# First pass of a fused retention, ELU and GLU kernel: one d_ff block of the first two half groups moved to the pass's end, retention two steps further ahead, four x stores issued by ScalarE

## The chip, the cores and the metric

The kernel runs on one core of one Trainium2 chip. The metric is the device time of one execution in microseconds (us). Engines are named as in the profile: PE (TensorE), DVE (VectorE), ACT (ScalarE), POOL (GpSimd), SP (SyncE). An engine works through its own instructions in the order in which they stand. The execution that was profiled is one execution; the times are the median of several.

## The reference, cut to what matters

```python
# retention: batch 4, heads 8, seq 576, head_dim 64
scores = q @ k.T / sqrt(64);  ret = scores * gamma_h ** (i - j)  (0 where j > i)
x = (ret @ v), heads side by side          # 2304 tokens x 512
h = x @ w_in                               # 512 -> 2048
x = where(h > 0, h, exp(min(h, 0)) - 1) @ w_out
gate = sigmoid(x @ w_gate)                 # 512 -> 1536
out = (gate * (x @ w_val)) @ w_out2
```

All weights come as 64-bit words (float64) and are turned into pairs of float32 on the chip. Every large product is made of three PE products of high and low parts.

## The kernel before

**Tokens and groups.** 2304 tokens are 18 retention steps of 128 tokens. Steps 0 to 3 make token group 0, 4 to 7 group 1, and so on; group 4 has two steps. A half group is 256 tokens, two steps. The 2048 columns of d_ff are 16 blocks of 128.

**First pass.** `FP = 2`: the first pass takes d_ff blocks 0 and 1 for all nine half groups, 18 FF steps `s` in the list `ff`. Step `s = 2j + f` is half group `j`, block `f`. `ff[s].ups` is 12 products on PE into a bank `h` (L369), then on ACT Relu and Exp (L382, L383), on DVE a combination (L386), on ACT the high part of the result `g` (L108) and on DVE or POOL its low part (L109). `ff[s - 2].downs` (`LAG = 2`) is 12 products into two accumulator banks (L113 to L115), and after the last block of a half group `evac` copies them to `y`.

**Retention.** Between the FF steps stands `block(n)`: on PE `inter` of step n, `scores` of step n + 1, `outs` of n, `sums` of n + 1, 64 products of 64x64 in float32, which are 128 matrix products and 128 weight loads in the trace (L263). On DVE follow `causal` (L275, the mask of scores n + 1), `x_mul` (L336, the output x of step n out of the bank `to`), the two halves of `states` (L297, L301, the state of step n + 1; POOL L302 and L260 scale it and the next v), and `x_low` (L350); ACT makes `x_high` (L343). `inter` of step n + 1 waits for the second half of `states`, so from one block to the next there is a chain PE, `x_mul`, `states`, PE. `x_low` also stores the float32 x of groups 0 to 3 to memory (L354), read again in later passes. `x_mul` of step n writes one of two tiles `e`, so it waits for the store of step n - 2.

**Weights.** `chain` of a Weight is five stages: two ACT operations (L153, L154), two DVE (L156, L157), DVE L160, DVE L162, then ACT L168 for the high part and DVE or POOL L171 for the low part. `stages(w, n)` runs n of them where it stands; in a FF step `stage()` does.

**Order.** It is written out by hand (`manual_schedule`). Before, `AHEAD = 2`: at step s from 4 on `block(s + 2)` runs ahead of `ups`; steps 0 to 3 have an order of their own, with warm-up products on PE (L121) in between. SP issues nearly all transfers, in program order; it also holds an empty instruction (L317) between `inter` and `outs` of a step, for which PE waits.

The second pass begins at s = 18 with group 4 and adds to the same `y`; later passes follow. The lines that set the order in the first pass:

```python
            if LATE <= s < NSTEP - AHEAD:
                block(s + AHEAD)
            ...
            ff[s].ups(stage, s, middle, end_)
            ...
            if s >= LAG:
                ff[s - LAG].downs(stage)
```

Of the kernel before, what the change touches and what calls it, by code (L numbers as in the profile page):

```python
# [24 lines left out]
NT = B * S  # L25
# [5 lines left out]
NSTEP = (B // 2) * NS  # L31
# [7 lines left out]
KEPT = 3  # L39
SEVEN = 5  # L40
N0 = 256
AHEAD = 2
LATE = 4
SPARE = {3: 2, 8: 2, 4: 3, 9: 3, 14: 3}
LAG = 2
WARM = 12, 2, 3, 5, 4, 6


LEAST = float(np.array(0x38000000, np.uint32).view(np.float32))
# [4 lines left out]
def retention_elu_glu(  # L54
# [25 lines left out]
    class Ring:  # L80
# [5 lines left out]
        def more(self, pool, n):  # L86
            self.homes += [(pool, f"{self.name}{len(self.homes) + i}") for i in range(n)]
# [87 lines left out]
    def t_slot(n, f):  # L175
        if n == "i":
            return f % 2 + 3 * (f > 5 and f % 4 < 2)
        return 2 if not f % 2 or f == 2 * Q0 + 1 else 0 if f == FA - 1 else 5

    W, weights = {}, []  # L180
    for f in range(FA):
        for n, src in (("i", w_in), ("o", w_out)):
            i = len(weights)
            W[n, f] = Weight(src[f], i % 8, (0, 0, 1, 1, 0, 1, 0, 1)[i] if i < 8 else t_slot(n, f))
            weights.append(W[n, f])


# [35 lines left out]
    class Step:  # L223
# [125 lines left out]
        def x_low(self):  # L349
            dve.tensor_tensor(out=self.x[1], in0=self.xf, in1=self.x[0].bitcast(F32), op=ALU.subtract)  # L350
            if self.g < 4:
                if not self.at:
                    whole[self.g] = dpool.tile([128, KB, 512], F32, tag=f"x{self.g}", name="x")
                sp.dma_start(out=whole[self.g][:, :, self.at : self.at + 128], in_=self.xf)  # L354


    class FF:
# [425 lines left out]
    with tc.manual_schedule():  # L783
# [33 lines left out]
        steps[0].load()  # L817
        weights[0].load()
        steps[1].load()
        weights[2].load()  # L820
        steps[2].load()
        steps[3].load()
        weights[1].load(raws[:, 0, :])
        steps[4].load()
        weights[3].load(raws[:, 1, :])

# [5 lines left out]
        def block(n, scales=True):  # L832

            more = n + 1 < NSTEP
            steps[n].inter()
            if more:
                steps[n + 1].scores()
            steps[n].outs()
            if more:
                steps[n + 1].sums()  # L840
                steps[n + 1].causal()
            for load in loads_at.get(n, []):
                load()
            steps[n].x_scaled()
            if more:
                steps[n + 1].states()
                if scales and n + 2 < NSTEP:
                    steps[n + 2].scale()
            steps[n].x_low()

        def stages(chain, n):
            for _ in range(n):
                next(chain)


        w0, w2 = weights[0].chain(dve, apart=True), weights[2].chain(dve)
        warm_up(WARM[0])
        steps[0].scale()
        steps[0].scores()
# [18 lines left out]
        steps[1].causal()  # L878
        steps[1].states()
        steps[0].x_low()  # L880
        stages(w2, 2)
        warm_up(3)
        steps[1].inter()
        steps[1].outs()
# [2 lines left out]
        steps[1].x_high()  # L887
        stages(w0, 1)
        steps[1].x_low()
        stages(w2, 2)  # L890
        for load in loads_at[1]:
            load()
        for X in range(2):
# [2 lines left out]


        passes = [list(range(f, f + FP)) for f in range(0, 2 * Q0, FP)]
        ff = [FF(0, j // 2, f, passes[0], j % 2 * N0, N0) for j in range(NT // N0) for f in passes[0]]
        begins = [0, len(ff)]  # L900
        ff += [FF(1, g, f, passes[1]) for g in (4, 2, 3, 0, 1) for f in passes[1]]
        end = len(ff)

        a, b = begins
        conv, loads = {2: weights[3]}, {}
        for i, w in enumerate(weights[4:8]):
            s = a + 6 + (i * (b - a - 6)) // 4
            conv[s] = w
# [147 lines left out]
        for s in range(end):  # L1056
            if halves is not None:
                next(halves, None)
            chain = halves = None
            if s in conv:  # L1060
                chain = halves = made[name_of[id(conv[s])]] = convert(conv[s])
                if conv[s] is W["i", 2 * Q0 + 2]:
                    halves = None
                if conv[s] is W["i", 2 * Q0]:
                    chain = halves = islice(chain, 4)
            if s == b:
                chain = made["i", 2 * Q0]

            def stage():
                if chain is not None:  # L1070
                    next(chain, None)
                if s >= begins[1] + 4:
                    next(prepared, None)
            stage()
            if LATE <= s < NSTEP - AHEAD:
                block(s + AHEAD)
            if s == NSTEP - AHEAD:
                more()
            middle = end_ = None
            if s == 0:  # L1080
                def middle():
                    stages(w2, 1)
                    steps[2].scores()
                    steps[2].sums(True)
                    steps[2].causal()

                def end_():
                    steps[2].states()
                    steps[3].scale()
                    steps[4].scale()  # L1090
            ff[s].ups(stage, s, middle, end_)
            if s == 1:
                w1 = weights[1].chain(dve)
                block(2, False)
                stages(w1, 2)
                warm_up(WARM[4])
                steps[3].inter()
                steps[4].scores()
                steps[3].outs()
                steps[3].x_mul()  # L1100
                steps[4].sums()
                steps[4].causal()
                steps[3].x_high()
                steps[5].scale()
                stages(w1, 1)
                steps[3].x_low()
                steps[4].states()
                stages(w1, 2)
                for load in loads_at.get(3, []):
                    load()  # L1110
                warm_up(WARM[5])
            if 1 < s < LATE:
                block(s + AHEAD)
            for w in loads.get(s, []):
                w.load()
            if s >= LAG:
                ff[s - LAG].downs(stage)
            else:
                stage()
            save()  # L1120
            for i, n in enumerate(("11", "21", "22")):
                if s == begins[1] + 2 + i:
                    second.store(n)
            if s == begins[1] + 8:
                park()
                more()
            if s == begins[1] + LAG - 1:
                ret.close()
                right = ctx.enter_context(tc.tile_pool(name="right", bufs=1, side="right"))
                e_tile.more(right, 3)  # L1130
                e_tile.n = 5
                g_tile.more(right, 2)
                t_tile.more(right, 1)
                s_tile = Ring("s", right, 2, [128, 2, 2, DM], F32R)
                ps_acc = ctx.enter_context(tc.tile_pool(name="ps_acc", bufs=1, space=bass.MemoryType.PSUM))
                ps_u = ctx.enter_context(tc.tile_pool(name="ps_u", bufs=1, space=bass.MemoryType.PSUM))
                acc_bank = Ring("acc", ps_acc, 4, [128, 512], F32)
                u_bank = Ring("u", ps_u, 2, [128, 512], F32)
# [296 lines left out]
```

## Time and profile before

| | us |
|---|---|
| runs | 889.15, 889.76, 886.13 (median 889.15) |
| profiled execution | 885.46 |
| its span, first to last instruction | 883.7 |
| PE busy in the span | 861.0 |
| DVE, ACT, POOL busy | 664.9, 460.1, 410.2 |

PE is busy for 97% of the span. The first pass, which the change rewrites, ends at about 123.5 us, where the products of the second pass's first step start; 760 us follow. The warm-up products count as busy PE but compute nothing.

### The profile page before, as it was taken

To read this page: it belongs to the slowest core of one execution; us is meant where nothing else is said; L and a number is where in the kernel's file an instruction comes from. 1 tells how busy PE (TensorE), PEld (TensorE's weight loads), DVE (VectorE), ACT (ScalarE), POOL (GpSimd) and SP (SyncE) were. 2 spreads that over 40 slices of the span, in tenths; PEclk is the share of its full clock that TensorE was granted. 3 is DMA by queue.
4 is the path that set the end of the run, shared out by engine and by line. 5 is a ranking of instruction groups with operands and counts; after the bars stand their busy time and mean duration, and the time that the engine had idled before them with its cause. 6 is when DMAs were issued, how large, how long until landed. Compare 5 with 4: busy or idle time off the path is not lost.

```text
span 883.7 us, 16178 instructions
## 1 busy us (share of the span) xinstructions
PE 861.0 (97%) x6370; PEld 729.2 (83%) x6375; DVE 664.9 (75%) x967; ACT 460.1 (52%) x833; POOL 410.2 (46%) x327
## 2 busy tenths in 40 slices
PE   7898999999999999999899999999999999999998
PEld 4798897788888888888788888888888888888886
DVE  5867649679999888887787989479966554786774
ACT  3445475677666656666564565455534334344331
POOL 2446435556556542555361566245434143334353
PEclk9999999999999999999999999999999999999999
DMA  9978528735565595997783766555565565554322
GB/s 342 295 229 271 151 57 311 300 121 190 191 197 209 214 402 201 329 354 273 279 329 113 258 232 227 194 187 186 200 243 186 197 232 194 211 211 179 114 117 96
DMA packets 63724, 194.83 MB, mean 220 GB/s; under 512 B 9760, under 2 KB 18976, under 8 KB 57248
## 3 DMA queue, kind: packets, MB, share of 16 engines
q1 hardware_dynamic: 62544, 192.31, 61.1%
q10 hardware_dynamic: 1104, 1.49, 0.5%
q8 instruction: 50, 0.82, 0.4%
q14 instruction: 26, 0.21, 0.1%
HBM read 127.19 MB, written 66.58 MB: 219 GB/s over the span
## 4 chain that ended last, share of the span: by engine, by line
PE 82%; DVE 8%; ACT 4%; DMA 3%; issue 2%; POOL 1%; SPq 0%; DVEq 0%; ACTq 0%; POOLq 0%
PE u L113 13%; PE u L115 13%; PE u L114 13%; PE acc L113 9%; PE acc L114 9%; PE acc L115 9%; PE tile L113 4%; PE tile L114 4%; PE tile L115 4%; PE to L263 3%; PE h L369 1%; DVE t L157 1%; DMA h<-x 1%; DVE t L156 1%; DMA raw<-in_w_in 1%
## 5 line engine op out<-in xcount | busy, mean ns | idle before, releaser
L109 POOL TENSOR_TENSOR g<-e,g 128x512 fp32r<-128x512 f32 x95 | 132.7, 1402 | 234.3 <-ACT g L108 219.8
L113 PE MATMUL u<-x,s 128*128 128x512 f32 x288 | 114.8, 398 | 3.0 <-DVE e L538 2.5
L115 PE MATMUL u<-x,s 128*128 128x512 f32 x288 | 114.5, 398 | 0.0
L114 PE MATMUL u<-x,s 128*128 128x512 f32 x288 | 114.1, 396 | 0.0
L113 PE MATMUL u<-x,w 128*128 128x512 f32 (+1 forms) x264 | 98.4, 373 | 0.5 <-DVE u L524 0.5
L114 PE MATMUL u<-x,w 128*128 128x512 f32 (+1 forms) x264 | 98.3, 372 | 0.0
L115 PE MATMUL u<-x,w 128*128 128x512 f32 (+1 forms) x264 | 97.8, 371 | 0.0
L108 ACT CAST g<-e 128x512 fp32r<-128x512 f32 x101 | 61.9, 620 | 60.7 <-DVE e L579 39.9
L171 POOL TENSOR_TENSOR w<-t,w 128x512 fp32r<-128x512 f32 x37 | 51.7, 1398 | 41.6 <-ACT w L168 38.9
L113 PEld LDWEIGHTS u<-x,s 128*128 128x128 f32 x288 | 54.3, 189 | 15.5 <-DVE e L538 3.1
L115 PEld LDWEIGHTS u<-x,s 128*128 128x128 f32 x288 | 54.4, 189 | 13.2
L114 PEld LDWEIGHTS u<-x,s 128*128 128x128 f32 x288 | 54.5, 189 | 12.0
L113 PE MATMUL acc<-g,w 128*128 128x512 f32 (+1 forms) x176 | 60.8, 345 | 2.5 <-ACT y L422 1.5
L114 PE MATMUL acc<-g,w 128*128 128x512 f32 (+1 forms) x176 | 60.2, 342 | 0.0
L115 PE MATMUL acc<-g,w 128*128 128x512 f32 (+1 forms) x176 | 60.1, 341 | 0.0
L776 DVE TENSOR_TENSOR y<-y,acc 128x512 f32<-128x512 f32 x58 | 39.1, 682 | 27.5 <-PE acc L115 27.3
L740 DVE TENSOR_TENSOR y<-y,tile 128x512 f32<-128x512 f32 x76 | 51.2, 680 | 10.5 <-PE tile L115 10.2
L113 PEld LDWEIGHTS u<-x,w 128*128 128x128 f32 x264 | 49.8, 189 | 9.4 <-DVE u L524 1.1
L115 PEld LDWEIGHTS u<-x,w 128*128 128x128 f32 x264 | 49.8, 188 | 9.0
L114 PEld LDWEIGHTS u<-x,w 128*128 128x128 f32 x264 | 49.9, 189 | 7.8
L656 DVE TENSOR_TENSOR y<-y,acc 128x512 f32<-128x512 f32 (+1 forms) x68 | 39.6, 606 | 19.7 <-PE acc L115 17.9
L114 PE MATMUL acc<-w,g 128*128 128x512 f32 (+1 forms) x152 | 54.4, 358 | 0.0
(216 smaller groups left out, 2410.0 us busy)
## 6 DMA issues: line engine op xcount, KB each, us to landing
w<-c SPq DMA_DIRECT2D x72, 512.0 KB, 6.4
c<-w SPq DMA_DIRECT2D x48, 512.0 KB, 4.9
s<-c SPq DMA_DIRECT2D x22, 1024.0 KB, 6.4
c<-s SPq DMA_DIRECT2D x18, 1024.0 KB, 4.9
in<-in_ain SPq DMA_DIRECT2D x12, 1024.0 KB, 7.4
y<-y SPq DMA_DIRECT2D x8, 1024.0 KB, 6.2
raw<-in_w_in SPq DMA_DIRECT2D x12, 512.0 KB, 5.4
c<-x SPq DMA_DIRECT2D x12, 512.0 KB, 6.8
```

The costliest lines, as they stand in the source:

```text
L108: act.copy(hi, src)
L109: lo_engine.tensor_tensor(out=lo, in0=src, in1=hi.bitcast(F32), op=ALU.subtract)
L113: pe.matmul(out_, wh, xh, start=start, stop=False, skip_group_check=shared)
L114: pe.matmul(out_, wh, xl, start=False, stop=False, skip_group_check=shared)
L115: pe.matmul(out_, wl, xh, start=False, stop=stop, skip_group_check=shared)
L156: dve.tensor_scalar(out=f, in0=f, scalar1=LEAST, scalar2=MOST, op0=ALU.max, op1=ALU.min)
L157: dve.tensor_scalar(out=u, in0=u, scalar1=5, scalar2=2, op0=ALU.logical_shift_left, op1=ALU.logical_shift_right)
L171: lo_engine.tensor_tensor(out=w[:, 1, :], in0=f, in1=w[:, 0, :].bitcast(F32), op=ALU.subtract)
L263: return pe.matmul(out_, w, x, start=start, stop=True, skip_group_check=True)
L656: dve.tensor_tensor(out=out_, in0=out_, in1=a, op=ALU.add)
L740: dve.tensor_tensor(out=y, in0=y, in1=a, op=ALU.add)
L776: dve.tensor_tensor(out=o, in0=o, in1=a, op=ALU.add)
```

## The change

The list `ff` now has block 0 alone for half groups 0 and 1 (steps 0 and 1), then both blocks for half groups 2 to 8 (steps 2 to 15), then block 1 for half groups 0 and 1 as two steps at the end (16 and 17), with pass number 2: their `evac` adds to `y` on DVE, 128x256 at a time, where the first pass copies on ACT. `AHEAD = 4`, so blocks 2 to 5 stand in steps 0 and 1, blocks 6 to 17 ahead of `ups` in steps 2 to 13, and none in steps 14 to 17. The weight converted ahead of the first FF step is now block 0 of w_out (w1) in place of block 1 of w_in (w2), and w1 is loaded before it; w2 follows in steps 0 and 1, w3 at step 3 in place of 2. Of two groups of warm-ups, of four and six, the one of four stays. The x stores of steps 0 to 3 are issued by ACT, behind `x_high`, and those of later steps by SP as before. One line fewer stands at the top, so a line of the change has a number lower by one down to the reordered part.

```diff
-AHEAD = 2
-LATE = 4
+AHEAD = 4
-WARM = 12, 2, 3, 5, 4, 6
+WARM = 12, 2, 3, 5, 4, 1
...
-                sp.dma_start(out=whole[self.g][:, :, self.at : self.at + 128], in_=self.xf)
+                (act if self.n < 4 else sp).dma_start(out=whole[self.g][:, :, self.at : self.at + 128], in_=self.xf)
...
         steps[1].load()
-        weights[2].load()
+        weights[1].load(raws[:, 0, :])
         steps[2].load()
         steps[3].load()
-        weights[1].load(raws[:, 0, :])
+        weights[2].load()
...
-        ff = [FF(0, j // 2, f, passes[0], j % 2 * N0, N0) for j in range(NT // N0) for f in passes[0]]
+        halves = lambda P, js, fs: [FF(P, j // 2, f, fs, j % 2 * N0, N0) for j in js for f in fs]
+        ff = halves(0, (0, 1), [0]) + halves(0, range(2, NT // N0), passes[0]) + halves(2, (0, 1), [1])
...
-            if LATE <= s < NSTEP - AHEAD:
+            if 1 < s < NSTEP - AHEAD:
                 block(s + AHEAD)
...
+            if s == 1:
+                block(4)
+                stages(w2, 1)
...
             ff[s].ups(stage, s, middle, end_)
+            if s == 0:
+                block(2, False)
+                warm_up(WARM[4])
+                block(3)
+                stages(w2, 2)
             if s == 1:
-                w1 = weights[1].chain(dve)
-                block(2, False)
-                stages(w1, 2)
-                warm_up(WARM[4])
-                steps[3].inter()
-                ...
-                warm_up(WARM[5])
-            if 1 < s < LATE:
-                block(s + AHEAD)
+                stages(w2, 2)
+                block(5)
```

On PE, behind the four warm-ups that follow block 2. Before, from `ups` of step 2 (`in_217` is the input of retention step 5, `y3` that of step 4):

```order
L369 MATMUL h_591<-x0_111,w_261 128x256 x12
L263 MATMUL to_99<-y3_109,y4_110 64x64 x16
L263 MATMUL ts_98<-in_217 64x64 x16
L263 MATMUL to_99<-a_560,y3_109 64x64 x16
L263 MATMUL to_99<-in_217 64x64 x16
L113 MATMUL acc0_691<-g_378,w_571 128x256
L114 MATMUL acc0_691<-g_378,w_571 128x256
```

In the change, from the last products of block 3 on:

```order
L262 MATMUL to_99<-y3_109 64x64 x16
L262 MATMUL to_99<-y3_109,y4_110 64x64 x16
L262 MATMUL ts_98<-in_217 64x64 x16
L262 MATMUL to_99<-a_533,y3_109 64x64 x16
L262 MATMUL to_99<-in_217 64x64 x16
L368 MATMUL h_635<-x0_111,w_261 128x256 x12
L262 MATMUL to_99<-in_217,y4_110 64x64 x16
L262 MATMUL ts_98<-in_314 64x64 x16
```

Block 4 stood between `ups` and `downs`; now it follows block 3 directly, and `ups` of step 1 comes behind it.

On DVE, from `x_mul` of one step to the states that the block after next waits for. Before, from `x_mul` of step 2 (`e_475`) to the states of step 4 (`t_483` is the weight w1):

```order
L336 TENSOR_TENSOR e_475<-to_99,cq_sb_100 128x2x4x64
L297 TENSOR_TENSOR y4_110<-st1_104,to_99 128x256
L301 TENSOR_TENSOR y4_110<-y4_110,to_99 128x256
L350 TENSOR_TENSOR x0_111<-e_475,x0_111 128x4x128
L156 TENSOR_SCALAR t_483<-t_483 128x512
L157 TENSOR_SCALAR t_483<-t_483 128x512
L336 TENSOR_TENSOR e_542<-to_99,cq_sb_100 128x2x4x64
L275 TENSOR_TENSOR a_560<-ts_98,tri_102 128x512
L160 ISA t_483<-y1_107,t_483 128x1024
L350 TENSOR_TENSOR x0_111<-e_542,x0_111 128x4x128
L297 TENSOR_TENSOR y4_110<-y4_110,to_99 128x256
L301 TENSOR_TENSOR st0_103<-y4_110,to_99 128x256
```

In the change, behind the states of step 5, from `x_low` of step 4 to the states of step 6 (`t_550` and `w_655` are the weight w2, `d_634` and `g_651` belong to `ups` of step 1):

```order
L349 TENSOR_TENSOR x1_112<-e_623,x1_112 128x4x128
L159 ISA t_550<-raw_106,t_550 128x1024
L385 SCALAR_TENSOR_TENSOR d_634<-d_634,h_635 128x256
L108 TENSOR_TENSOR g_651<-d_634,g_651 128x256
L161 SCALAR_TENSOR_TENSOR t_550<-raw_106,t_550 128x512
L170 TENSOR_TENSOR w_655<-t_550,w_655 128x512
L274 TENSOR_TENSOR a_723<-ts_98,tri_102 128x512
L335 TENSOR_TENSOR e_727<-to_99,cq_sb_100 128x2x4x64
L296 TENSOR_TENSOR y4_110<-st0_103,to_99 128x256
L300 TENSOR_TENSOR y4_110<-y4_110,to_99 128x256
```

Three stages of w2 and two operations of a FF step stand between `x_low` of step 4 and `x_mul` of step 5.

On ACT, from the cast of the first weight on. Before:

```order
L168 CAST w_261<-t_168 128x512
L299 COPY y4_110<-to_99 128x256
L153 ACTIVATE t_271<-raw_106 128x512
L154 ACTIVATE raw_106<-raw_106 128x512
L343 CAST x0_111<-e_306 128x4x128
L168 CAST w_338<-t_271 128x512
L382 ACTIVATE d_324<-h_325 128x256
```

In the change:

```order
L167 CAST w_261<-t_168 128x512
L298 COPY y4_110<-to_99 128x256
L353 DMA x_269<-e_220 512x1x128
L152 ACTIVATE t_271<-y1_107 128x512
L153 ACTIVATE y1_107<-y1_107 128x512
L342 CAST x0_111<-e_306 128x4x128
L353 DMA x_269<-e_306 512x1x128
L381 ACTIVATE d_324<-h_325 128x256
L382 ACTIVATE d_324<-d_324 128x256
L167 CAST w_379<-t_271 128x512
```

The stores of steps 0 and 1 stand ahead of the second weight's two operations and of the first Relu.

## Rows read from the trace of the kernel before

**Rows 1.** Busy time by stage: us, busy (instructions) of each engine, clock, DMA share, GB/s.

```profile
18.90:54.40 35.50, 31.32 (x904) 28.24 (x906) 26.76 (x49) 13.98 (x31) 16.37 (x17) 1.00 0.95 292
54.40:123.50 69.10, 63.94 (x1472) 60.98 (x1467) 45.12 (x79) 36.73 (x89) 30.04 (x33) 1.00 0.60 186
```

**Rows 2.** Timeline of PE: start, us, engine, line, operation, count [idle before, releaser].

```profile
24.07 0.27 PE L263 MATMUL to<-in,y 64*64 64x64 f32 x1 [0.75 <-DVE y L301]
...
26.30 0.65 PE L263 MATMUL to<-y 64*64 64x64 f32 x32
...
29.46 0.27 PE L263 MATMUL to<-y,y 64*64 64x64 f32 x1 [1.54 <-DVE y L301]
...
33.65 1.24 PE L121 MATMUL h<-y 128*128 128x512 bf16 x5 [0.16 <-issue]
...
54.41 1.70 PE L369 MATMUL h<-x,w 128*128 128x256 f32 x12
...
57.48 0.73 PE L263 MATMUL to<-y,y 64*64 64x64 f32 x17
```

**Rows 3.** Timeline of DVE, second weight and the first retention blocks.

```profile
20.23 0.69 DVE L162 SCALAR_TENSOR_TENSOR t<-raw,t 128x512 uint32<-128x512 uint32 x1
21.61 0.69 DVE L171 TENSOR_TENSOR w<-t,w 128x512 fp32r<-128x512 f32 x1 [0.68 <-ACT w L168]
22.22 0.68 DVE L275 TENSOR_TENSOR a<-ts,tri 128x512 f32<-128x512 f32 x1
22.82 0.41 DVE L386 SCALAR_TENSOR_TENSOR d<-d,h 128x256 f32<-128x256 f32 x1
...
27.93 0.69 DVE L336 TENSOR_TENSOR e<-to,cq_sb 128x512 f32<-128x512 f32 x1 [1.22 <-PE h L121]
28.54 0.41 DVE L297 TENSOR_TENSOR y<-st,to 128x256 f32<-128x256 f32 x1
28.98 0.42 DVE L301 TENSOR_TENSOR y<-y,to 128x256 f32<-128x256 f32 x1
29.32 0.68 DVE L350 TENSOR_TENSOR x<-e,x 128x512 fp32r<-128x512 f32 x1
```

**Rows 4.** Timeline of ACT, the first FF step.

```profile
20.96 0.62 ACT L168 CAST w<-t 128x512 fp32r<-128x512 f32 x1 [2.09 <-DVE t L162]
21.48 0.38 ACT L382 ACTIVATE d<-h 128x256 f32<-128x256 f32 x1
21.89 0.42 ACT L383 ACTIVATE d<-d 128x256 f32<-128x256 f32 x1
23.26 0.40 ACT L108 CAST g<-d 128x256 fp32r<-128x256 f32 x1 [0.95 <-DVE d L386]
```

**Rows 5.** Transfers issued by SP: timeline of two x stores.

```profile
13.96 3.98 SPq L354 DMA_DIRECT2D x<-e  x1
...
28.65 0.56 SPq L354 DMA_DIRECT2D x<-e  x1
```

**Rows 6.** Transfers issued from 13.9 to 16 us: count, KB each, us to landing.

```profile
x<-e SPq DMA_DIRECT2D x1, 256.0 KB, 13.9
```

**Rows 7.** PE's waits, 54 to 124 us: us in total, times, longest.

```profile
PE h L369 <- ACT x L343: 2.5, 1, 2.5
PE acc L113 <- ACT y L422: 1.5, 2, 0.9
PE to L263 <- DVE st L301: 0.6, 1, 0.6
PE to L263 <- issue: 0.4, 1, 0.4
```

**Rows 8.** DMA queue for PE's instructions: packets, MB, share; whole span, then 83.2 to 83.6 us.

```profile
q8 instruction: 50, 0.82, 0.4%
...
q8 instruction: 1, 0.02, 16.0%
```

**Rows 9.** Busy time, columns as in rows 1, between two waits of PE.

```profile
85.50:91.20 5.70, 5.26 (x128) 4.99 (x128) 2.26 (x3) 1.21 (x3) 3.35 (x4) 1.00 0.73 271
```

More of the change, by code (lines that the diff above doesn't have):

```diff
@@ L183, in retention_elu_glu @@
             i = len(weights)
-            W[n, f] = Weight(src[f], i % 8, (0, 0, 1, 1, 0, 1, 0, 1)[i] if i < 8 else t_slot(n, f))
+            W[n, f] = Weight(src[f], i % 8, (0, 1, 0, 1, 0, 1, 0, 1)[i] if i < 8 else t_slot(n, f))
             weights.append(W[n, f])
@@ L853, in stages @@
                 next(chain)
-        w0, w2 = weights[0].chain(dve, apart=True), weights[2].chain(dve)
+        w0, w1, w2 = weights[0].chain(dve, apart=True), weights[1].chain(dve), weights[2].chain(dve)
         warm_up(WARM[0])
@@ L880, in retention_elu_glu @@
         steps[0].x_low()
-        stages(w2, 2)
+        stages(w1, 2)
         warm_up(3)
@@ L889, in retention_elu_glu @@
         steps[1].x_low()
-        stages(w2, 2)
+        stages(w1, 2)
         for load in loads_at[1]:
@@ L904, in retention_elu_glu @@
         a, b = begins
-        conv, loads = {2: weights[3]}, {}
+        conv, loads = {3: weights[3]}, {}
         for i, w in enumerate(weights[4:8]):
@@ L1074, in retention_elu_glu @@
             stage()
-            if LATE <= s < NSTEP - AHEAD:
+            if 1 < s < NSTEP - AHEAD:
                 block(s + AHEAD)
-            if s == NSTEP - AHEAD:
+            if s == NSTEP - AHEAD + 1:
                 more()
+            if s == 1:
+                block(4)
+                stages(w2, 1)
             middle = end_ = None
@@ L1081, in middle @@
                 def middle():
-                    stages(w2, 1)
                     steps[2].scores()
@@ L1088, in end_ @@
                     steps[2].states()
+                    stages(w1, 1)
                     steps[3].scale()
@@ L1091, in retention_elu_glu @@
             ff[s].ups(stage, s, middle, end_)
-            if s == 1:
-                w1 = weights[1].chain(dve)
-                block(2, False)
-                stages(w1, 2)
-                warm_up(WARM[4])
-                steps[3].inter()
[L1098 to L1110, printed above, removed]
-                warm_up(WARM[5])
-            if 1 < s < LATE:
-                block(s + AHEAD)
+            if s == 0:
[3 more added lines that the diff above has]
+                stages(w2, 2)
+            if s == 1:
+                stages(w2, 2)
+                block(5)
             for w in loads.get(s, []):
```

## The prediction

> **What bounds the kernel now.** I began with busy time by stage [rows 1]. The change rewrites the first pass, so the stages are cut where it matters: 18.9 us is the start of `ups` of step 0, 54.4 us the moment when blocks 0 to 7 are done, 123.5 us the end of the pass. The granted clock is 1.00 throughout, so nothing here is a matter of the clock. From 18.9 to 54.4 PE is idle for 35.50 - 31.32 = 4.2 us, and about 2 us of its busy time are warm-ups; DVE is busy for 26.8 of 35.5. From 54.4 to 123.5 PE is idle for 5.2 us. So PE bounds the pass, with some 11 us of slack in it, and PE's useful work is the same in both kernels: 18 `ups`, 18 `downs`, 18 blocks. What the change can win or lose is idle PE, and the place to look is the wait that ends last between one block and the next.
>
> The timeline of PE shows that place [rows 2]. Block 2 runs from 24.07 to 26.95, that is 2.9 us; the next one starts at 29.46, after four warm-ups and 1.54 us of nothing, released by the second half of `states`. The timeline of DVE [rows 3] shows the chain in between: `x_mul` at 27.93, then 28.54 and 28.98 for the two halves, end 29.40: 1.5 us, and with the hand-overs 1.6 us from the end of one block to the start of the next, if DVE is free. A FF step put between two blocks hides it: `ups` and `downs` together take 57.48 - 54.41 = 3.07 us [rows 2], 1.54 each.
>
> Two more things show in the rows. `x_mul` at 27.93 is put down to a warm-up product [rows 3], which makes no data for it. The true releaser is the store of step 0's x, issued at 13.96 and 13.9 us on its way [rows 5, 6]: 27.9. And the longest PE wait after 54.4, 2.5 us, names an ACT cast [rows 7]; that cast writes the x of step 12, while the product that waits reads steps 10 and 11. It ends at 85.6. Inside it a packet of PE's instruction queue runs [rows 8], and PE then executes exactly 128 + 128 = 256 instructions up to the next wait, which has no releaser at all [rows 7, 9]. The queue moved 50 packets of 16 KB for 12,745 matrix products and weight loads, 255 each. So I read both waits as PE waiting for its next 256 instructions. A block is 128 products and 128 loads, so a packet that holds one block and nothing else is used up in 2.6 us.
>
> **The change part by part: steps 0 and 1.** I follow PE from 18.9 us, which stays, to the end of block 7.
>
> Block 2. Ahead of the states of step 2, DVE did the low part of the second weight and waited 0.68 for its cast [rows 3]. Now `causal` and the FF operation come first and the low part follows the states; ACT does Relu and Exp ahead of the cast [rows 4]. `causal` 21.15 to 21.8, L386 to 22.2, the two halves to 23.0: block 2 starts at 23.05 in place of 24.07. PE idles for 1.35 us instead of doing `ups` of the old step 1.
>
> Blocks 2 to 5, without the instruction supply. Block 2 ends at 25.95. The store of step 0 is out of the way: ACT issues it at about 14.7, behind no other store, so `x_mul` starts at once; block 3 starts at 27.55 and ends at 30.45. Block 4, which used to follow `ups` and precede `downs`, now follows directly: 32.05 to 34.95. Then `ups` of step 1 hides one turn: block 5 from 36.55 to 39.45.
>
> Block 6. Here DVE has the most queued. Between the end of block 4, when `x_mul` of step 4 can start, and the states of step 6 it does, by the order in front of this text: `x_mul` 0.69, the two halves 0.77, `x_low` 0.65, L160 0.65, L386 0.41, g's low part 0.41, L162 0.65, w's low part 0.65, `causal` 0.65, `x_mul` 0.69, the two halves 0.77 [rows 3]; they overlap a little, so each is taken a little under its duration, L160 as L162 and g's low part as L386. That is 7.0 us. Twice it waits for ACT, for g's cast, 0.45, and for w's cast, 0.65 [rows 4]; the 0.68 ahead of L171 [rows 3] is such a wait. With hand-overs 8.2 us: 34.95 + 8.2 = 43.2. PE has block 5 done at 39.45, so it idles for 3.7 us. This is the largest term, and nothing can cover it: block 6 is next on PE and `ups` of step 2 stands behind it.
>
> Block 6 ends at 46.1, `ups` of step 2 at 47.6, `downs` of step 0 at 49.15. Block 7 (its step 8 makes no sums) takes 2.0 us, as before: 51.15. Before, block 7 was done at 54.4, but with two `ups` and two `downs` more, 2 x 3.07 = 6.1 us. So on equal work the change stands at 57.3: **+2.8 us**. The removed six warm-ups (1.24 us with their gap [rows 2]) and the removed wait for the store are in this figure already.
>
> The instruction supply. From 18.9 to 54.4 PE got through 904 + 906 instructions [rows 1], 5.0 us per 256. The change has about 110 fewer there, 1,700 or 6.6 packets: at the same rate 33.2 us, to 52.1, which is 1.0 us later than the walk. Bounds: nothing, if no packet is late; 2.5 us at the 5.7 us that 256 instructions took from 85.5 to 91.2 [rows 9]. I take **+1.0**.
>
> On this the Trainium skill speaks otherwise (Runtime: NRT & Kernel Launch, Instruction fetch mechanics): the sequencer fetches the next 16 KiB block of 256 instructions while it executes the current one, and a boundary is "mostly hidden". No idle 2.5 us fits that; by the page this term and the supply waits below would be nothing, and the sum +3.1 in place of +3.3.
>
> The x stores. SP no longer holds four of them, and ACT does. In rows, an issue takes between 0.56 us (28.65) and 3.98 us (13.96) of the issuing engine [rows 5]. I take 0.56 for ACT, since the long ones stand where SP's own backlog was largest; ACT has time for that, as its first reader, the Relu, starts 0.9 us later anyway. The upper end is the second rival. The Trainium skill (DMA: Bandwidth & Descriptors, Queues, rings and completion order) gives SP and ACT a ring each on every DMA engine, served in turn. By that ACT would not stand behind SP's backlog, as in the forecast; no row here shows an ACT issue during it.
>
> **From there to the end of the pass.** Each step with a block is PE work as before. Of the 5.2 us idle, 2.9 are supply [rows 7], 1.5 `downs` waiting for `evac`, 0.8 states and a scaled v. In the change no packet is a block alone; two hold 238 and 244 instructions of blocks (about 3.4 us of work in place of 2.6), which by the 5.1 us of the packet at 83 (2.55 of work and 2.55 of waiting) makes about 0.9 each: 1.8. The rest stays 2.3, with 0.3 more for the two further steps without a block, where `evac` has less cover. 4.4 in place of 5.2: **-0.8**. Bounds: -4.4 if nearly all of it goes, +1 if a packet again meets a block alone.
>
> The two moved steps at the end add eight times 128x256 on DVE where ACT copied; at 0.42 [rows 3] 1.7 us a step. The products of the next step hide it, for `downs` comes 1.5 us of `ups` later and needs the first two of four. I take **+0.3** for the rest; without that cover 1.7.
>
> Sum: 2.8 + 1.0 - 0.8 + 0.3 = +3.3 us. The profiled execution took 885.46 us (span 883.7, 1.8 around it), so the change would take 888.8 there; the median of the runs lies 3.7 us higher, at 889.15, and the same sum gives **892.4 us**.
>
> **The rivals.**
>
> 1. *The late waits go.* The retention is done at step 13, so ACT and DVE are free in the last steps and `evac` comes in time, and no packet is late. The start costs 3.8 as above, the 5.2 us of idle shrink to 0.8: 889.15 + 3.8 - 4.4 + 0.3 = 888.9. For it: the evac waits stand where a block and a weight meet. Against: the two supply waits come from blocks, which stay.
>
> 2. *ACT is held by its stores (slower).* If ACT's issue takes what SP's took, 3.98 at 14.65, the second weight's operations start at 18.6 in place of 14.5, and DVE has their follow-up ahead of `x_mul` of step 1: it starts at 20.2 in place of 17.5, +2.7 on the retention chain. The second store (2.3 us over the 0.56) holds Relu and Exp, and L386 stands ahead of the states on DVE: +1.3. It decides as soon as an issue takes over 1 us. 892.4 + 4.0 = 896.4. For it: the memory system is busy for 0.95 of that stage [rows 1]. Against: ACT's transfers run on a queue of their own.
>
> 3. *Start and end both come out low.* No packet is late at the start either, and DVE's wait for the two casts overlaps: +2.3 in place of 3.8, with rival 1's end: 887.3, and down to 884 if DVE's chain to block 6 is 3 us shorter than its rows add up to.
>
> **How the numbers follow.** A measurement of this kernel can tell about 0.5% from no change, 4.4 us, so from 884.7 to 893.6. Forecast 0.45, of it 0.12 above 893.6; rival 1 0.22, within; rival 2 0.18, slower; rival 3 0.15, about half of it faster. Faster 0.08, same 0.62, slower 0.30. The range runs from 886.5 to 896.5: below lies part of rival 3, above the worst of rival 2. The forecast's own range, by its bounds, is 890 to 895.
>
> **What would show it.** Right: block 2 starts about 1 us earlier; `x_mul` of step 2 waits for nothing but its block; PE idles for 3 to 4 us ahead of block 6, and DVE is busy there with w2; block 7 is done near 52; the pass ends 3 us later than before. Wrong: ACT's store issues of several us (rival 2); idle after 54 us of under 2 us (rival 1); no gap ahead of block 6 (rival 3); or a difference that arises after 123.5 us, for which I have no term.

## The result

The change makes the kernel slower: 896.62 us (median of 6 runs, 893.01 to 898.61) against 887.05 (6 runs). The ratio on record is 1.0096, 95% interval 1.0076 to 1.0116; the two medians alone give 1.0108, inside the interval. The forecast was 892.4, at most 896.5, so the median lies 0.12 us above the top of the range. The profiled execution took 894.57 us, its span 892.8: 9.1 us more than the span of before.

Busy time by stage, columns as in [rows 1]. Blocks 0 to 7 are done at 55.6 us, the first pass ends at 130.7. The last two rows are stretches of the first.

```profile
18.90:55.60 36.70, 26.40 (x851) 24.23 (x850) 23.70 (x43) 10.78 (x24) 14.04 (x14) 0.91 0.89 291
55.60:130.70 75.10, 69.83 (x1512) 66.57 (x1513) 46.82 (x85) 41.16 (x101) 32.81 (x36) 1.00 0.58 169
...
35.00:40.00 5.00, 4.71 (x118) 4.59 (x118) 2.40 (x5) 0.62 (x1) 0.12 (x1) 0.66 0.88 209
46.00:50.00 4.00, 3.39 (x108) 3.39 (x110) 1.61 (x4) 0.43 (x1) 1.94 (x2) 0.57 0.53 174
```

Up to block 7 PE idles for 10.3 us, where it idled for 4.2, and its granted clock is below 1.00 in two stretches, which it never was in [rows 1]. Two `ups` and two `downs` (6.1 us) that stood in this stretch now come later, so on equal work the change stands at 55.6 + 6.1 = 61.7 against 54.4: **+7.3 us**. From there to the end of the pass PE idles for 5.3 us, as before (5.2): nothing is won or lost. The other 1.8 of the 9.1 us arise behind the pass.

Timeline of PE, columns as in [rows 2]: blocks 2, 3, 4 (twice), 6, then `ups` of steps 2 and 3 and the rest of block 8.

```profile
22.70 0.27 PE L262 MATMUL to<-in,y 64*64 64x64 f32 x1 [1.46 <-DVE y L300]
...
28.82 0.21 PE L262 MATMUL to<-y,st 64*64 64x64 f32 x1 [0.72 <-issue]
...
32.35 0.85 PE L262 MATMUL to<-y,y 64*64 64x64 f32 x21 [1.57 <-DVE st L300]
...
35.29 0.39 PE L262 MATMUL to<-y,y 64*64 64x64 f32 x7 [2.09 <-issue]
...
46.61 0.37 PE L262 MATMUL to<-in,y 64*64 64x64 f32 x1 [3.60 <-DVE y L300]
...
50.44 1.70 PE L368 MATMUL h<-x,w 128*128 128x256 f32 x12
...
55.52 1.70 PE L368 MATMUL h<-x,w 128*128 128x256 f32 x12
...
63.99 0.38 PE L262 MATMUL to<-y 64*64 64x64 f32 x9 [2.13 <-issue]
```

Two kinds of waits stand here. Those for DVE are the chain of the forecast. Those marked "issue", with no releaser, stand in the middle of a block, one (0.6) in a group of `downs`. Block 4 begins at 32.35, is held for 2.09 us at 33.20 and needs another 2.93 us for what is left of it. PE's waits from 18.9 to 130 us, columns as in [rows 7]:

```profile
PE to L262 <- DVE y L300: 5.7, 3, 3.6
PE to L262 <- issue: 4.9, 3, 2.1
PE acc L112 <- ACT y L421: 1.6, 1, 1.6
PE to L262 <- DVE st L300: 1.6, 1, 1.6
PE h L368 <- ACT x L342: 0.9, 1, 0.9
PE acc L113 <- issue: 0.6, 1, 0.6
```

DVE's chain ahead of block 6, as in [rows 3], and ACT's four x stores:

```profile
38.26 0.69 DVE L335 TENSOR_TENSOR e<-to,cq_sb 128x512 f32<-128x512 f32 x1 [1.01 <-PE to L262]
...
43.88 0.69 DVE L170 TENSOR_TENSOR w<-t,w 128x512 fp32r<-128x512 f32 x1 [0.68 <-ACT w L167]
...
46.14 0.42 DVE L300 TENSOR_TENSOR y<-y,to 128x256 f32<-128x256 f32 x1
```

```profile
14.09 0.61 ACTq L353 DMA_DIRECT2D x<-e  x1
...
17.80 0.57 ACTq L353 DMA_DIRECT2D x<-e  x1
...
26.45 0.52 ACTq L353 DMA_DIRECT2D x<-e  x1
...
31.98 0.53 ACTq L353 DMA_DIRECT2D x<-e  x1
```

**Where the packets are.** PE's instructions come in 50 packets [rows 8]. For each longer wait without a releaser (0.35 us or more, from 18.9 to 130 us) I counted the products and weight loads that PE had begun before it. In the eight traces that miss no record the count leaves 183 to 189 on division by 256; in the other six, which miss up to five products, 178 to 185. I call that a crossing, and the 256 behind it a piece. PE crosses at 51.50 us, in `ups` of step 2. The transfers by queue from 51.5 to 55.9 us, then from 55.9 to 57 (q1 data, q8 PE's instructions: packets, MB, share):

```profile
q1 hardware_dynamic: 914, 1.19, 92.4%
...
q1 hardware_dynamic: 104, 0.09, 44.3%
q8 instruction: 1, 0.02, 5.5%
```

For 4.4 us behind the crossing the engines move 1.2 MB of data and no instruction packet; then one comes, takes 0.97 us, and PE's next crossing, which it reaches at 57.70, is passed at 58.28, 1.37 us after the packet's end. So a piece takes at least delay + 0.97 + 1.4 us. From 28.82 to 63.99 PE passes six pieces, 5.9 us each; in the kernel before it passed seven from 30.06 to 64.22, 4.9 us each. Of the 35 us in the change 5.2 are waits for DVE.

### The profile page after: what moved, and what is told of

It reads as the page before. It is cut to its first block, busy times and chain, and to the rows that moved or that the text cites. A ratio compares the mean times of both kernels' runs of the same rounds, so it can differ in the third digit from the quotient of the medians.

```text
span 892.8 us, 16173 instructions
## 1 busy us (share of the span) xinstructions
PE 863.0 (97%) x6365; PEld 731.3 (82%) x6369; DVE 668.9 (75%) x975; ACT 460.9 (52%) x833; POOL 409.5 (46%) x327
## 4 chain that ended last, share of the span: by engine, by line
PE 76%; DVE 6%; ACT 2%; DMA 1%; issue 1%; DVEq 0%; ACTq 0%; SPq 0%
PE u L112 13%; PE u L113 13%; PE u L114 13%; PE acc L112 8%; PE acc L113 8%; PE acc L114 8%; PE tile L112 4%; PE tile L113 4%; PE tile L114 4%; DVE y L423 1%; DMA raw<-in_w_o 1%; DVE t L156 1%; DVE t L159 1%; DVE t L155 1%; PE h L368 0%
## 5 line engine op out<-in xcount | busy, mean ns | idle before, releaser
L113 PE MATMUL acc<-w,g 128*128 128x512 f32 (+1 forms) x152 | 54.4, 358 | 0.0
```

The costliest lines, as they stand in the source:

```text
L113: pe.matmul(out_, wh, xl, start=False, stop=False, skip_group_check=shared)
```

## The experiments

Theory A, as it stood after the comparison: besides DVE's chain, the late packets (5.5 us in all, 3.2 in the kernel before) and the low clock behind idle stretches make up the loss; blocks that follow each other use up 256 instructions in 4.5 us, faster than a packet comes behind the loads. Twelve kernels were run besides the two; the table has all of them, with the sum of PE's waits marked "issue" in the first pass (18.9 to 130 us; for before, before_act and before_split the misnamed wait near 83 us is added):

| kernel | ratio to before, 95% | "issue" waits, us |
|---|---|---|
| before | 1 | 3.2 |
| the change | 1.0096 (1.0076 to 1.0116) | 5.5 |
| before_act | 1.0008 (0.9995 to 1.0022) | 6.4 |
| sp_stores | 1.0071 (1.0053 to 1.0089) | 5.9 |
| w2_late | 1.0104 (1.0079 to 1.0128) | 8.4 |
| shifted | 1.0079 (1.0063 to 1.0096) | 6.0 |
| gap_warm | 1.0085 (1.0062 to 1.0109) | 8.4 |
| downs_early | 1.0064 (1.0041 to 1.0087) | 9.3 |
| downs_early_w2 | 1.0086 (1.0056 to 1.0117) | 7.8 |
| more_load | one execution, 907.09 us | 8.1 |
| no_loads | one execution, 890.97 us | 2.4 |
| split_loads | 1.0047 (1.0033 to 1.0062) | 4.1 |
| before_24 | 0.9991 (0.9976 to 1.0007) | 4.0 |
| before_split | 0.9991 (0.9976 to 1.0005) | 1.0 |

The waits are those of one execution of each kernel, which need not be its median: that of sp_stores took 900.45 us (median 895.0), that of split_loads 893.48 (median 891.84), that of the change 894.57 (median 896.62).

### before_act and sp_stores: the stores alone

```diff
-                sp.dma_start(out=whole[...], in_=self.xf)
+                (act if self.n < 4 else sp).dma_start(out=whole[...], in_=self.xf)
```

(before_act; sp_stores is the reverse edit in the change.)

> The kernel before with this part of the change alone: x stores of steps 0 to 3 by ACT. Theory A (the store of step 0 holds x_mul of step 2 until 27.93): x_mul of step 2 starts about 0.9 us earlier, the next block at 28.6 in place of 29.46, and up to 0.9 us of that reaches the end: ratio 0.999 to 1.000. Rival (ACT held by its issues): ratio over 1.001, first Relu later than 20.96.

> The change with the x stores of steps 0 to 3 issued by SP again. Theory A (ACT's store issues cost 0.5 to 0.6 us each and hold nobody, and the early landing of step 0's store is worth its wait): x_mul of step 2, at 25.7 us in the change, waits for the store of step 0 until about 28, so everything behind is 1.5 to 2.3 us later: ratio 1.011 to 1.012. Rival (ACT's issues or its transfers are a part of the loss): 1 us or more faster than the change, ratio under 1.009, and fewer idle us on PE ahead of 35 us.

Timeline of before_act: `x_mul` of step 2 on DVE, then PE's block 3 and the wait in it.

```profile
26.20 0.69 DVE L336 TENSOR_TENSOR e<-to,cq_sb 128x512 f32<-128x512 f32 x1
...
27.72 0.27 PE L263 MATMUL to<-y,y 64*64 64x64 f32 x1 [0.64 <-DVE y L301]
...
29.75 0.27 PE L263 MATMUL to<-y,y 64*64 64x64 f32 x1 [1.53 <-issue]
```

The store's landing was the wait: `x_mul` starts at 26.20 in place of 27.93, block 3 at 27.72 in place of 29.46. And 0.5 us into it PE waits for its next piece until 29.75. The gain of 1.7 us is gone within the block, and the kernel is not faster. In sp_stores the reverse: `x_mul` of step 2 starts at 28.14 and block 3 2.4 us later than in the change, as theory A said, and SP, held by its own issues, keeps PE another 1.88 us in block 2; but at the end of block 4 only 0.75 us are left of it, since there the wait is 1.00 in place of 2.09. My 1.011 was wrong; the ratio of 1.0071 does not make ACT's stores a gain, and its interval overlaps that of the change, so they are no proven loss either.

### w2_late: DVE's chain made shorter

```diff
             if s == 1:
-                stages(w2, 2)
                 block(5)
+                stages(w2, 2)
```

> The change, with the last two stages of w2 (its low half and its split) behind block 5 instead of ahead of it, so that DVE comes to causal of step 6, x_mul of step 5 and the states of step 6 without them. Theory A (DVE's queue sets the start of block 6, and PE's idle time there is followed by a stretch of low granted clock): in the change PE idles 3.60 us ahead of block 6 and block 6 then takes 3.9 us in place of 2.9. Here the idle time falls to about 1.6 us and block 6 takes 2.9 again: 2.9 us less than the change, ratio to the kernel before 1.006. Theory B (the queue alone, the clock has another cause): 2.0 us less, block 6 still 3.9, ratio 1.007. Theory C (a supply wait or another producer comes right behind): idle time over 3 us stays, ratio 1.010.

Timeline of PE: the first products of block 6, the last of `ups` of step 2, the rest of block 8.

```profile
45.33 0.27 PE L262 MATMUL to<-in,y 64*64 64x64 f32 x1 [1.77 <-DVE y L300]
...
51.39 0.62 PE L368 MATMUL h<-x,w 128*128 128x256 f32 x3 [1.57 <-issue]
...
63.93 0.38 PE L262 MATMUL to<-y 64*64 64x64 f32 x9 [2.96 <-issue]
```

The idle time ahead of block 6 fell from 3.60 to 1.77, and block 6 started 1.3 us earlier. Then three products short of the end of `ups` a wait of 1.57 appears that the change hadn't, and block 8 goes on at 63.93, in the change at 63.99. Ratio 1.0104: nothing gained. Behind the shorter gap block 6 ran at a granted clock of 1.00 (45.3 to 48.5 us), as theory A said; the low clock behind block 4 lasted until 40.5 us, in the change until 39.4. Theory C held in its outcome, by the supply.

### shifted and before_24: moving the pieces against the program

```diff
-        warm_up(WARM[0])
+        warm_up(6)
+        narrow = h_bank()
+        for _ in range(38):
+            pe.matmul(narrow[:, :32], warm[:, :128], warm[:, :32], start=True, stop=True)
```

(before_24: `warm_up(9)` and 15 narrow ones in the kernel before.)

> The change with 64 PE instructions more ahead of the first retention step (38 narrow warm-up products in place of six wide ones, while PE waits for its first input), so that every later piece of 256 PE instructions ends 64 instructions earlier in the program. Theory A (the waits of 0.72, 2.09, 0.59 and 2.13 us at 28.1, 33.2, 57.7 and 61.9 us, which have no releaser, are PE waiting for its next 256 instructions): all four disappear from their places inside a block or a down product, what is left of them stands 64 instructions earlier, where it partly overlaps the wait for DVE between two blocks; the pass is 1 to 3 us shorter, ratio to the kernel before 1.006 to 1.009. Theory B (they belong to the products that wait, by data that the profile doesn't name): they stay at the same products, ratio 1.010.

> The kernel before with 24 PE instructions more at its start (15 narrow warm-up products in place of three wide ones, while PE waits for its first input), so that the pieces of 256 end 24 instructions earlier in the program: the piece that was exactly one block (80.5 to 83.1 us, then 2.54 us of waiting) now holds 24 instructions of a FF step, about 1.6 us of work, and 232 of the block. Theory A (a wait at a piece's end is 5.1 us from the piece's start to the next one's arrival, less the time that its instructions take): the wait at 83 us falls by 1 to 1.6 us, and with other waits of up to 0.5 us moving either way the ratio is 0.998 to 1.000. Theory B (the wait belongs to the product, not to the count): 2.5 us ahead of the same product, ratio 1.000.

Timeline of PE in shifted, then the wait of before_24:

```profile
28.43 0.39 PE L262 MATMUL to<-y 64*64 64x64 f32 x7 [1.53 <-issue]
...
34.35 0.45 PE L262 MATMUL to<-y 64*64 64x64 f32 x11 [0.72 <-issue]
...
45.92 0.92 PE L262 MATMUL to<-in 64*64 64x64 f32 x23 [1.82 <-issue]
...
92.85 0.27 PE L262 MATMUL to<-y 64*64 64x64 f32 x1 [1.70 <-issue]
```

```profile
85.97 0.45 PE L263 MATMUL to<-in 64*64 64x64 f32 x12 [2.28 <-issue]
```

No wait stands at its old product, each stands where the count says; theory B is out. In before_24 the 2.54 us that stood ahead of `h` [rows 7] now stand within the block ahead of it, and as nothing there waits for ACT they read "issue". But the sum did not fall: 6.0 against 5.5 us in shifted (from 46 to 91 us no wait without a releaser, but a new one at 92.85), 2.28 in place of 2.54 in before_24, where I expected 1 to 1.6 less. Its packet started about 4 us after the crossing near 79.5, in the kernel before 2.7 us after that at 80.5. The arrival is not a fixed 5.1 us after a piece's start.

### no_loads and more_load: what the packets stand behind

```diff
+            again = {7: 2, 9: 6, 10: 5, 11: 6, 12: 5, 13: 6, 14: 5, 15: 6, 16: 5}.get(self.n)
+            if again:
+                self.t = steps[again].t
...
+            if again:
+                return
```

(no_loads, in `load`; below more_load, in the loop over FF steps.)

```diff
+            if 5 <= s <= 12:
+                for _ in range(2):
+                    sp.dma_start(out=dpool.tile([128, 1024], I32, ...), in_=weights[4].src.bitcast(I32))
```

> The change without the input loads of retention steps 7, 9 to 16 (1 MB each): those steps compute on the tiles of steps 2, 5 and 6 again, so what they compute is not the reference's; PE, DVE, ACT and POOL do the same work in the same order. From about 25 us on the DMA engines carry only the stores of x, the weights and two more inputs. Theory A (PE's packets of 256 instructions are late because they stand behind the loads): from 40 us on a packet starts under 2 us after PE has begun the piece before (in the change 4.4 at 51.5 and 3.3 at 58.3), the waits of 0.59 and 2.13 us at 57.7 and 61.9 go, and the first pass ends 3 us or more sooner. Theory B (the loads don't set it): packets as late as in the change, the wait in block 8 stays at about 2 us.

> The change with 1 MB of transfers more in each of the FF steps 5 to 12 (two copies of a 512 KB weight in memory to an unused place, issued by SP), about 70 to 110 us, where the change shows no wait for instructions: there a packet of PE's queue starts 0.6 to 2.4 us after PE has begun the piece before, in 46 to 62 us it starts 3.3 to 4.4 us after. Theory A (a packet stands behind the other transfers of its DMA engine): in 70 to 115 us packets start 3 us or more after, and waits of 0.5 to 2.5 us without a releaser appear at the products where a piece of 256 ends. Theory B (what delays a packet is not the load of the DMA engines): starts and waits in 70 to 115 us stay as they are.

PE's waits in no_loads up to 130 us, the first and second line:

```profile
PE to L267 <- DVE y L305: 4.7, 3, 2.6
PE to L267 <- issue: 2.1, 2, 1.3
```

Its queues behind the same crossing, at about 48.3: until 49.2 no packet of any queue moves; from 49.2 to 50.3 us:

```profile
q1 hardware_dynamic: 447, 0.23, 70.4%
q8 instruction: 1, 0.02, 5.4%
```

Without the loads the packet starts at 49.27, about 1 us after this crossing, where it took 4.4 in the change, and from 39 us to the end of the retention no product waits for instructions. Block 7 is done at 52.6 in place of 55.6, and the pass's last wait, for `evac`, begins at 112.7 in place of 118.7; the one execution is 3.6 us shorter than that of the change. With more load the reverse: from 74 to 117 us packets start up to 4.0 us after the crossing, six of eight 2.7 or more (in the change 0.7 to 2.4), and waits of 1.0, 0.5 and 1.1 us appear at crossings. Theory A by both. The 12.5 us that more_load lost against the change are not all supply: its waits for DVE, ACT and SP come to 14.0 us from 18.9 us to the end of the pass, in the change to 9.8, and its granted clock averages 0.92 there; I can't say what of this the added transfers caused.

### gap_warm: the clock

```diff
                 stages(w2, 2)
                 block(5)
+                warm_up(14)
```

> The change with 14 warm-up products on PE behind block 5, in the 3.6 us in which PE waits for DVE ahead of block 6; nothing else is changed, and block 6 can start no earlier. Theory A (the granted clock falls to its lower level because PE stands idle there): the rows from 46 to 50 us show 1.00 in place of 0.50, block 6 takes 2.9 us in place of 3.9, and what lies behind it starts 0.9 us earlier. Theory B (the clock falls for another reason, for instance by a pattern in the program's time): block 6 still takes 3.9 us, and nothing is gained. The ratio to the kernel before can hardly tell 0.9 us: 1.007 to 1.010 by either; the rows decide.

Busy PE, granted clock, DMA share, GB/s of gap_warm from 46 to 50 us:

```profile
46.00:50.00 4.00, 3.44 (x131) 1.00 0.47 140
```

In the change this stretch ran at 0.57 on average, with whole microseconds at 0.50, the lower of the two levels (1.2 GHz). With products in the 3.6 us of idle time it runs at 1.00 (2.4 GHz), and block 6 takes 3.1 us besides a wait of 0.47 in it, in place of 3.9. So the fall is due to the idle stretch. The other executions agree: in all five that leave PE idle for 2.65 to 3.60 us ahead of block 6 (the change, more_load, no_loads, sp_stores, split_loads) the granted clock falls to 0.50 in the gap or in block 6; in w2_late, with 1.77, it stays at 1.00 there. Again the time was not gained: waits of 0.47, 1.01 and 1.96 follow, and behind the last one the clock falls here, where the change had 1.00:

```profile
64.00:69.00 5.00, 5.00 (x36) 0.66 0.54 151
```

### downs_early and downs_early_w2: FF work between the blocks

```diff
                 block(3)
+                ff[0].downs(stage)
                 stages(w2, 2)
             if s == 1:
                 stages(w2, 2)
                 block(5)
+                ff[1].downs(stage)
-            if s >= LAG:
+            if s >= LAG + 2:
```

> The change with `downs` of steps 0 and 1 put where PE waits: that of step 0 between blocks 3 and 4, that of step 1 behind block 5, ahead of block 6; steps 2 and 3 then have none. The work is the same. Theory A (blocks that follow each other directly wait for DVE's chain and use up 256 PE instructions faster than they arrive; products of a FF step between them cover both): the 1.57 and 2.09 us ahead of and in block 4 shrink by at least 1.6 together, the 3.6 us ahead of block 6 become about 2, block 6 runs at full clock; 3 to 5 us less than the change, ratio 1.004 to 1.006. Rival (the supply is only paid later, since blocks 6, 7 and 8 now have one group of 12 products between them in place of two): waits of 1 to 3 us appear in blocks 7 to 9, under 1.5 us is gained, ratio over 1.008.

> The same, with the last two stages of w2 behind block 5 as well, so that `downs` of step 1 covers the whole of DVE's chain ahead of block 6. Theory A: the idle time ahead of block 6 falls under 0.5 us, 1 to 2 us less than with `downs` moved alone, ratio 1.002 to 1.005. Rival (supply): the 1 to 2 us come back as a wait for the next 256 instructions between 45 and 65 us, ratio as with `downs` moved alone.

PE's longest waits without a releaser: downs_early, in blocks 4 and 5, then downs_early_w2, in `ups` of steps 1 and 3.

```profile
35.27 0.74 PE L262 MATMUL to<-y,y 64*64 64x64 f32 x19 [2.44 <-issue]
...
45.20 0.48 PE L262 MATMUL to<-in 64*64 64x64 f32 x3 [2.84 <-issue]
```

```profile
40.94 0.51 PE L368 MATMUL h<-x,w 128*128 128x256 f32 x3 [2.62 <-issue]
...
58.04 1.65 PE L368 MATMUL h<-x,w 128*128 128x256 f32 x8 [3.12 <-issue]
```

The waits for DVE between 32 and 62 us are gone in both, 5.2 us in the change (1.57 and 3.60). In their place stand supply waits, 9.3 and 7.8 us in the pass. About 3 us may be won in downs_early (1.0064), the intervals just overlap; the second edit adds nothing (1.0086). Neither half of the expectation came out whole: the supply waits came back as the rival said, and the ratio of downs_early lies nearer to theory A.

### split_loads and before_split: smaller loads

```diff
-                sp.dma_start(out=self.t, in_=src)
+                sp.dma_start(out=self.t[:, :2], in_=src[:, :2])
+                rest.append(lambda: sp.dma_start(out=self.t[:, 2:], in_=src[:, 2:]))
```

The second half is issued at the end of the FF step.

> The change with the 1 MB input load of each retention step from 7 on issued as two halves: the first where the whole stood, the second at the end of that FF step. The bytes are the same. Theory A (a packet of PE's queue stands behind the load that was issued just ahead of it): the longest starts between 40 and 65 us, 4.4 and 3.3 us behind the crossing, fall to 1 to 3 us, the waits of 0.59 and 2.13 us at 57.7 and 61.9 fall by 1 us or more together, ratio to the kernel before 1.006 to 1.009. Rival (only the bytes count, not how they are bundled): the same waits in sum, ratio 1.009 to 1.010.

> The kernel before with the same halving of the input loads from step 7 on. Theory A: the packet that started 2.7 us behind its crossing at 80.5 comes sooner, the wait of 2.54 us at 83 falls by 0.5 to 2 us, ratio 0.997 to 0.999, the fastest of all kernels here. Rival: waits as before, ratio 1.000.

PE's waits of split_loads up to 130 us, then the wait of before_split that was 2.54 us:

```profile
PE to L267 <- DVE y L305: 5.2, 3, 3.1
PE to L267 <- issue: 3.3, 5, 0.9
...
PE h L373 <- issue: 0.8, 1, 0.8
```

```profile
85.11 1.70 PE L374 MATMUL h<-x,w 128*128 128x256 f32 x12 [0.61 <-ACT y L427]
```

This is the edit that pays: the same bytes in halves, and the change takes 1.0047 in place of 1.0096, the intervals apart. Half of the loss is gone with no other work moved; the two profiled executions differ by 1.1 us only, so the rows below show a part of it. The wait of 2.09 us in block 4 is 0.72, that of 2.13 in block 8 is 0.62. In the first pass the clock is at its lower level once (46 to 49 us, behind DVE's 3.1 us) and not twice.

The plainest rows are those behind the crossing that PE passes at 28.8 us, up to which the change, split_loads and no_loads do the same on PE: there the load of step 7 stands just ahead, whole, halved, and left out. From there to the start of the packet the DMA engines moved, in the change (3.64 us), split_loads (2.69) and no_loads (1.04):

```profile
DMA packets 1229, 1.40 MB, mean 384 GB/s; under 512 B 241, under 2 KB 664, under 8 KB 1229
DMA packets 1268, 0.98 MB, mean 364 GB/s; under 512 B 487, under 2 KB 946, under 8 KB 1268
DMA packets 574, 0.35 MB, mean 336 GB/s; under 512 B 145, under 2 KB 494, under 8 KB 574
```

The packet starts later the more bytes stand ahead of it, in these three executions. The halving also moves half of the bytes to a later time, so these runs don't show whether the size of a load matters by itself.

In the kernel before, the wait at 83 us fell from 2.54 to 0.61 as expected, but 0.9991 (0.9976 to 1.0005) can't be told from no change. No kernel here is measurably faster than the one before.

## Why the prediction was right or wrong

**The number: nearer than the reasons.** The forecast difference was 3.3 us; measured are 9.6 between the medians and 9.1 between the profiled executions. The time of 892.4 missed by 4.2 only because its base, a median of 889.15 from three runs, is 887.05 over six. And that 896.62 lies next to the top of the range is luck: the top stood for rival 2, which did not come. The bounds of the terms, taken together, give 887.9 to 897.2, and not the 890 to 895 that the forecast named as its own range.

**Start, the walk: right.** Block 2 starts at 22.70 (forecast 23.05), `x_mul` of step 2 at 25.72 behind its own block alone, block 3 at 27.25 (27.55), block 4 at 32.35 (32.05). From the end of block 4, 38.22, to block 6, 46.61, DVE's chain takes 8.4 us (8.2), and PE idles for 3.60 (3.7). In no_loads block 7 is done at 52.6; the forecast was 51.15 without supply and 52.15 with it, and that run still has 2.1 us of supply waits.

**Instruction supply: the step that failed by size.** I took 1.0 and at most 2.5. Ahead of block 7 it is 0.72 + 2.09 = 2.8. The bound was also wrongly worked out: 6.6 packets at 5.7 us end some 5.5 us behind the walk, not 2.5. I had the rate of before, 5.0 us per 256 instructions, as if a packet came by the clock. A packet's delay goes by what was queued just ahead of it, and three blocks in a row leave it 4.5 us a piece (2.9 for the block and 1.6 for the chain), where FF steps between them gave time. The row on which I could have built this was at hand: 5.1 us for the packet of 1 us at 83 us.

**The clock: the step that was missing.** "The granted clock is 1.00 throughout, so nothing here is a matter of the clock" was true of before alone. The change makes idle stretches of 3.7 us (1.57 and 2.09, with 0.85 of work between) and 3.6, and the rows behind each are at the lower level. What is left of block 4 takes 2.93 in place of 2.05, block 6 3.90 in place of 2.95: 1.8 us. Supply beyond the 1.0 and clock together make 1.8 + 1.8 = 3.6 us that the sum did not have; the start missed by 7.3 - 3.8 = 3.5. Over the runs, the mean granted clock is 0.991 in the change (6 runs) and 0.994 to 0.995 in four sets of runs of the kernel before; over 890 us that is 2 to 4 us, if PE had work all the time, so it can't settle the 1.8.

**Later waits: wrong, -0.8 forecast, 0.1 measured.** The two waits for packets came to 0.59 + 2.13 = 2.7 in place of 1.8, the two for `evac` and a late cast to 2.5 in place of 2.6. Their packets could be used 6.8 and 5.7 us after the crossings ahead of them, not 5.1. The 1.8 itself is a slip: 5.1 us less 3.4 us of work leaves 1.7 us of waiting for each, not 0.9, so the two come to 3.4, the term to +0.8 and the whole sum to 4.9. The measured 2.7 lies between.

**Moved steps: smaller than forecast.** The DVE adds left no wait that shows: the pass ends 7.2 us late, block 7 stood 7.3 late (0.3 forecast).

**After the pass: no term, and 1.8 us in this trace.** One wait for DVE near 441 us took 3.5 us where it took 2.5. Ahead of it a cast on ACT waits for a transfer, 8.5 us after that one's issue, before 7.2. Over the kernels the wait is 3.4 to 3.5 us in eight of the ten that have the change's order, 2.4 to 3.0 in the four of the other. I made no run for it; it and the other 0.8 us stay open.

**Rivals.** Rival 2 did not come: ACT's issues took 0.52 to 0.61 us as taken. The Trainium skill (DMA: Bandwidth & Descriptors, Queues, rings and completion order) has a ring of its own for ACT's transfers; by that they don't stand behind SP's backlog, and the trace agrees in that the first landed 9.8 us after its issue, by SP 13.9 [rows 6]. Rivals 1 and 3 failed on the same late packets. The sentence of the Trainium skill that speaks against the supply term (Runtime: NRT & Kernel Launch, Instruction fetch mechanics, "mostly hidden") would have put the sum at 3.1 in place of 3.3, farther off. It holds behind the first pass, where packets come some 26 us apart and no wait of PE lacks a releaser; not where a piece lasts under 6.

## What to carry to other kernels

Where PE runs many small products, look at the waits without a releaser and count its instructions: if the waits come every 256, the engine is paced by instruction packets that stand behind your own transfers, and a gain made just ahead of one is taken back at the next. Issuing large loads in parts paid here (split_loads); mixing such a stretch with large products (downs_early) removed the waits for the producer, but a gain in time is not shown. When a change makes PE idle for some microseconds, price the granted clock behind the gap too, from a row where it fell.

## What the runs showed of the hardware

Where PE waited for a packet of 256 instructions behind 50 us (two waits in each of the two kernels), it could use it 5.1 to 6.8 us after the crossing before; the packet itself took about 1 us. It started about 1 us after the crossing near 48.3 us when the loads were left out, and up to 4.0 us after when 1 MB a step was added to a stretch that had 0.7 to 2.4. Loads of 1 MB issued as two halves some microseconds apart cut the waits without a releaser from 5.5 to 4.1 us. A wait of 2.1 us was followed by the lower clock at 33 us and not at 62 us, and one of 2.3 us near 85 us was followed by it in before_act, one of 2.5 us at 83 us not in the kernel before; so the length of one wait alone does not decide it; with products in the gap it did not fall.
